# An interleaved local and block attention kernel: stacks, local scores and half-chunk sums each moved in fewer DMAs, in an order found anew

## The chip, the cores and the metric

The kernel runs on one core of one Trainium2 chip. A core has a TensorE (PE in the profile; its weight loads are listed apart as PEld), a VectorE (DVE), a ScalarE (ACT), a GpSimd (POOL) and a SyncE (SP). In this kernel SP issues most DMAs and ACT the rest; each of the two has a DMA queue of its own, and all transfers run on the core's 16 DMA engines. The metric is the device time of one execution in microseconds (us), as the median of several runs.

## What is computed

Four layers work in turn on x (2048 rows of 512, float32): A, B, A, B. Each is x + attention(layernorm(x)), with 32 heads of 16.

```python
def _A_ref(x, wqkv, wo):            # W, dil = 8, 2
    idx = pos[:, None] - off[None, :]        # off = arange(8) * 2
    ...
    logits = jnp.einsum("bhsd,bhswd->bhsw", q, kg) * scale
    attn = _softmax(logits, axis=-1)
    o = jnp.einsum("bhsw,bhswd->bhsd", attn, vg)

def _B_ref(x, wqkv, wo):            # W = 256
    scores = jnp.einsum("bhqd,bhkd->bhqk", q, k) * (Dh ** -0.5)
    mask = (idx[:, None] - idx[None, :] >= 0) & (idx[:, None] - idx[None, :] < W)
    p = _softmax(jnp.where(mask[None, None], scores, -1e9), axis=-1)
    o = jnp.einsum("bhqk,bhkd->bhqd", p, v)

x = x + _A_ref(_layernorm(x), A_wqkv, A_wo)
x = x + _B_ref(_layernorm(x), B_wqkv, B_wo)
x = x + _A_ref(_layernorm(x), A_wqkv, A_wo)
x = x + _B_ref(_layernorm(x), B_wqkv, B_wo)
```

## The kernel before

**Tiles and stages.** The 2048 rows are worked in 8 chunks of 256 (C = 256), so that the four layers make 16 A-chunks and 16 B-chunks. They are interleaved: while one B-chunk computes its scores on PE, the next A-chunk is projected and scored.

**An A-chunk** projects Q and K, computes the scores of 39 neighbouring rows for each group (`WIN` = 39) in two halves, and ScalarE copies each half from PSUM to a tile `s` of 128 x 1248 float32 (L1202). `shelve` (L1211) writes `s` to a DRAM tile `sd`, and `band` (L1215) reads it back along a diagonal into the tile `l`, where only the 8 wanted neighbours of each row are left. The probabilities go over DRAM too (`ptd`, `ptt`, L1285) before they meet V.

**A B-chunk** projects K, then Q, each in two halves. ScalarE takes a high float16 part `eh` from PSUM (L1331) and VectorE the remainder `el` (L1334). These have 128 partitions (4 groups of 32) with even and odd heads apart. To multiply high and low parts in one pass, the rows of a head's high, low and high part must lie in neighbouring partitions, so they are sorted anew through a DRAM tile `re`: six writes for K and six for Q in each B-chunk (`put`, L1344, 128 KB each), and then reads into the stacks `stk_q` (L1357) and `stk_k` (L1359). There are four stacks of Q and four of K in a chunk (`j` = 0 to 3, a pair of half `hf` and quarter `hp`); each is two DMAs of 48 rows, for even and odd heads, and waits for all six writes of its side. Rows 48 to 63 and 112 to 127 of the stacks are pads, written once at the start by 12 DMAs (`stk_k<-pad`, `stk_q<-pad`); two rows of the pads of Q are filled in every chunk with the maxima of the scores (`md`, L1471 and L1477).

The first scores, on 48 rows (L1404 in the first chunk of a layer, L1420 after), only serve to find the maxima on VectorE (L1435). The second (L1571), on 64 rows, contain the maxima as a subtraction, so that ScalarE takes their exponential straight from PSUM (L1581, L1593). GpSimd masks (L1610), PE multiplies by V with a column of ones (L1626), and the sums `os` hold each head's output and its denominator. `gather` (L1700) fetches the denominators of a half chunk into `rc`, VectorE inverts them, `scr` (L1710) and `os` (L1715) spread them over DRAM, and `gather_o` (L1705) fetches the outputs into `oc`.

**What sets the order.** Every piece of work is a task of the planner: an engine, a duration, a function that emits its instructions, and the values that it reads and writes. The dictionary `ORDER` gives each task of a chunk ("A0", "B0", and so on) a place; a negative place puts it on its other engine, which for DMAs is ACT for SP. Each engine gets its tasks sorted by place, the planner lays them out against each other by its own durations, and the instructions are emitted in that order. On the chip each engine executes its list strictly in that order: a DMA that waits for its data keeps back all that stands behind it on SP or ACT, and a matmul that waits keeps back all of PE. The planner gives a DMA a cost by its bytes alone, `dma = max(dma, t.end + 0.9) + t.size / 390.0`. At the start, PE also runs `IDLE` = 122 groups of matmuls that compute nothing (L1763).

Of the kernel before, what the change touches and what calls it, by code (L numbers as in the profile page):

```python
# [18 lines left out]
P = 128  # L19
S = 2048  # L20
# [660 lines left out]
def kernel(  # L681
# [456 lines left out]
    def layer_a(l, c):  # L1138
# [42 lines left out]
        for t in range(2):  # L1181
# [18 lines left out]
            for i in range(2):  # L1200
                def keep(i=i, S_=S_, pbs=pbs):
                    nc.scalar.copy(S_.t.rearrange("p k (s r) -> p r s k", r=4)[:, 2 * i : 2 * i + 2],  # L1202
                                   pbs[i].t[:, :, 0 : 8 * WIN].rearrange("p r (s k) -> p r s k", s=8))

                plan.add("ACT", 1.15, keep, r=[vpb[i]], w=[vS[i]])
            sd = buf("dram", [4, 32 * (WIN + 1) * H], F32, "sd", f"sd{l}_{c}_{t}")
            vsd = Val(sd)

            def shelve(E, S_=S_, sd=sd):
# [595 lines left out]
```

## Time and profile before

| what | before |
|---|---|
| time, median of 3 runs | 1408.19 us (1407.26 to 1411.21) |
| the profiled execution | 1414.15 us, of which the span of the profile is 1412.4 us |
| granted TensorE clock in it | 0.974 |
| PE matmul / weight load busy | 93% / 60% |
| DVE, ACT, POOL busy | 60%, 58%, 29% |
| DMA traffic | 195.08 MB in 203658 packets, mean 138 GB/s |

The profile covers one execution. In the chain of work that ended last, each step is followed back to what released it; "SPq" and "ACTq" are the times that the sequencers of SP and ACT took to issue a DMA, "DMA" the time from issue to landing. In a timeline, a row gives the start in us, the duration in us, the engine, the line of the kernel, the operation and its tiles as out<-in, and how many instructions are summed in the row; what an instruction waited for stands in square brackets. In a table of windows there is, for each stretch, the busy time and number of instructions of each engine, then the granted clock, the mean busy share of the 16 DMA engines, and GB/s.

### The profile page before, as it was taken

How to read it: one execution, taken by the hardware profiler on the slowest of the kernel's cores; microseconds unless marked ns; L12 is line 12 of the kernel's file. 1: busy time of each engine (PE TensorE's matmuls, PEld its weight loads, DVE VectorE, ACT ScalarE, POOL GpSimd, SP SyncE). 2: the span in 40 equal slices, each digit the busy share in tenths (PEclk: the TensorE clock that was granted, in tenths of full speed). 3: DMA queues.
4: the chain of work that ended last, by engine and by line, in shares of the span. 5: the costliest groups of instructions: out<-in, count | busy, mean ns of one | idle time of the engine just before them, and what ended most of it. 6: DMA issues, size and time to landing. Idle time of an engine off the chain costs nothing.

```text
span 1412.4 us, 62375 instructions
## 1 busy us (share of the span) xinstructions
PE 1308.5 (93%) x27206; PEld 841.8 (60%) x27206; DVE 852.2 (60%) x1932; ACT 825.8 (58%) x1303; POOL 405.9 (29%) x839
## 2 busy tenths in 40 slices
PE   8989999999898999879999898989999898998988
PEld 7766556575475746646566464746656474574645
DVE  5455764755647666374664637566473765748494
ACT  7754657474574746546676373838557364663644
POOL 5260212332221233133223130323242241222232
PEclk9999999999899998999999999999999999999999
DMA  8875544736355373552545546364554636335332
GB/s 261 236 168 162 133 115 135 154 114 171 102 148 134 88 200 92 148 147 86 160 113 152 152 143 158 94 174 125 157 123 134 175 100 155 102 98 147 103 98 67
DMA packets 203658, 195.08 MB, mean 138 GB/s; under 512 B 92892, under 2 KB 147932, under 8 KB 203384
## 3 DMA queue, kind: packets, MB, share of 16 engines
q1 hardware_dynamic: 175096, 170.43, 44.2%
q10 hardware_dynamic: 28288, 20.66, 6.0%
q8 instruction: 213, 3.49, 1.1%
q14 instruction: 61, 0.50, 0.1%
HBM read 94.11 MB, written 79.36 MB: 123 GB/s over the span
## 4 chain that ended last, share of the span: by engine, by line
PE 59%; DMA 11%; DVE 10%; ACT 7%; SPq 4%; issue 4%; POOL 2%; ACTq 1%; DVEq 0%; POOLq 0%
PE banks L1034 7%; PE banks L1626 7%; PE banks L1035 6%; PE banks L1036 6%; PE banks L1056 5%; PE banks L1054 5%; PE banks L1571 4%; PE banks L1057 4%; PE banks L1420 4%; DVE m L1435 3%; PE banks L1193 3%; PE banks L1302 3%; ACT p L1581 2%; DMA stk_q<-re 2%; DVE banks L1439 1%
## 5 line engine op out<-in xcount | busy, mean ns | idle before, releaser
L1435 DVE TENSOR_REDUCE m<-banks 128x2 f32<-128x512 f32 x448 | 302.1, 688 | 8.4
L1581 ACT ACTIVATE p<-banks,sclB 128x896 f32<-128x896 f32 x224 | 221.0, 1007 | 74.3 <-PE banks L1571 51.5
L1439 DVE COPY_PREDICATED banks<-trm,banks 128x128 f32<-128x128 int16 x448 | 124.2, 291 | 120.8 <-PE banks L1420 111.8
L1610 POOL TENSOR_SCALAR_AFFINE_SELECT ps<-ps 64x256 f32<-64x256 f32 x300 | 118.2, 416 | 252.3 <-ACT ps L1593 231.2
L1610 POOL TENSOR_SCALAR_AFFINE_SELECT p<-p 64x256 f32<-64x256 f32 x264 | 103.1, 412 | 214.7 <-ACT p L1581 206.6
L1420 PE MATMUL banks<-stk_k,stk_q 48*64 48x320 f16 (+4 forms) x2560 | 139.5, 274 | 24.5 <-DVE m L1435 7.0
L1571 PE MATMUL banks<-stk_q,stk_k 64*64 64x256 f16 (+3 forms) x3584 | 121.0, 239 | 25.0 <-DMA stk_q<-md 8.4
L1420 PEld LDWEIGHTS <-stk_q 48*64 48x64 f16 x2560 | 65.7, 107 | 107.5 <-issue 94.8
L1571 PEld LDWEIGHTS <-stk_k 64*64 64x64 f16 x3584 | 70.3, 108 | 91.0 <-issue 74.3
L1593 ACT ACTIVATE ps<-banks,sclB 128x768 f32<-128x768 f32 x112 | 100.2, 899 | 40.7 <-PE banks L1571 28.4
L1626 PE MATMUL banks<-p,v 64*32 64x192 f32 (+1 forms) x3584 | 112.6, 355 | 6.1 <-ACT p L1581 1.8
L1202 ACT COPY s<-banks 128x624 f32<-128x624 f32 x64 | 74.7, 1257 | 40.7 <-PE banks L1193 23.1
L1640 DVE TENSOR_TENSOR os<-os,banks 128x256 f32<-128x256 f32 x112 | 45.7, 416 | 83.4 <-ACT os L1643 67.0
L1334 DVE SCALAR_TENSOR_TENSOR el<-banks,eh 128x512 f16<-128x512 f32 x64 | 42.8, 687 | 79.4 <-ACT eh L1331 74.0
L1626 PEld LDWEIGHTS banks<-p,v 64*32 64x32 f32 x3584 | 62.9, 106 | 37.6 <-issue 13.0
L1643 ACT COPY os<-banks 128x256 f32<-128x256 f32 x112 | 40.8, 370 | 70.6 <-PE banks L1626 54.4
L1034 PE MATMUL banks<-xh,wA1h 128*128 128x256 f16 x256 | 72.1, 282 | 4.1 <-ACT v L1369 4.1
L1034 PE MATMUL banks<-xh,wA0h 128*128 128x256 f16 x256 | 71.9, 281 | 0.6 <-ACT v L1369 0.6
L1035 PE MATMUL banks<-xl,wA1h 128*128 128x256 f16 x256 | 71.7, 280 | 0.0
L1036 PE MATMUL banks<-xh,wA1l 128*128 128x256 f16 x256 | 71.5, 279 | 0.0
L1035 PE MATMUL banks<-xl,wA0h 128*128 128x256 f16 x256 | 71.3, 279 | 0.0
L1036 PE MATMUL banks<-xh,wA0l 128*128 128x256 f16 x256 | 71.1, 278 | 0.0
(216 smaller groups left out, 3063.8 us busy)
## 6 DMA issues: line engine op xcount, KB each, us to landing
sd<-s SPq DMA_DIRECT2D x92, 156.0 KB
ptt<-ptd SPq DMA_DIRECT2D x128, 96.0 KB
stk_k<-re SPq DMA_DIRECT2D x128, 96.0 KB
stk_q<-re SPq DMA_DIRECT2D x128, 96.0 KB
vs<-vd SPq DMA_DIRECT2D x64, 156.0 KB
re<-eh SPq DMA_DIRECT2D x75, 128.0 KB
vd<-ve SPq DMA_DIRECT2D x32, 256.0 KB
xm<-y SPq DMA_DIRECT2D x32, 256.0 KB
```

What stands on the lines that cost most here:

```text
L1034: nc.tensor.matmul(ps[mp].t[:, i], wh, xh, start=k == 0, stop=False)
L1035: nc.tensor.matmul(ps[mp].t[:, i], wh, xl, start=False, stop=False)
L1036: nc.tensor.matmul(ps[mp].t[:, i], wl, xh, start=False, stop=k == 3)
L1202: nc.scalar.copy(S_.t.rearrange("p k (s r) -> p r s k", r=4)[:, 2 * i : 2 * i + 2], pbs[i].t[:, :, 0 : 8 * WIN].rearrange("p r (s k) -> p ...
L1420: nc.tensor.matmul(o, lhs, k, start=True, stop=True, tile_position=(64 * par, 64 * h))
L1435: nc.vector.tensor_reduce(out=m.t[:, :, u, qb], in_=ps.t[:, :, 0 : 2 * P], op=ALU.max, axis=AX.X)
L1439: nc.vector.copy_predicated(t[:, :, 0:64], trm[:, 0].bitcast(I16).unsqueeze(1).broadcast_to([P, 2, 64]), t[:, :, C : C + 64])
L1571: nc.tensor.matmul(ps.t[64 * h : 64 * h + 64, par, at + x0 : at + x0 + q1 - q0], stk[hf, kt][r, col, k0 : k0 + 64], stk[hf, 0][r, col, q0: ...
L1581: nc.scalar.activation(big.t[:, 2 * i : 2 * i + 2], ps.t[:, :, 0:448], AF.Exp, scale=scl["B", 1])
L1593: nc.scalar.activation(small.t.rearrange("p (i m) x -> p m i x", i=2), ps.t[:, :, 0:384].rearrange("p m (i x) -> p m i x", i=2), AF.Exp, s ...
L1610: E.affine_select(out=v, in_=v, pattern=[[0, 4], [a, 64]], compare_op=op, fill=0.0, base=0, channel_multiplier=-a)
L1626: nc.tensor.matmul(acc.t[32 * mm : 32 * mm + 32, h, q0:q1], vv[r, 17 * (H * blk + hd) : 17 * (H * blk + hd) + 32], x.t[r, mm, x0 : x0 + q1 ...
```

## The change

Three transfers and their order are changed; what PE computes stays the same.

- **Stacks and pads.** The DRAM tile `re` of 3 parts by 2 halves becomes a ring of three permanent tiles for Q and three for K, of 4 stacks x 2 (even, odd) x 64 rows x 1024. Rows 48 to 63 of each hold the pads, written once at the start (6 DMAs in place of 12). A stack is one DMA of 128 rows with the pads (256 KB) in place of two of 48 rows (96 KB each). The writes of `put` are as many as before (12 in a B-chunk, 128 KB each), but what was in DRAM 64 rows of 2 pieces is now 4 stacks of 32 pieces.
- **Local scores.** `shelve` writes all 128 rows in one DMA instead of four of 32; `band` reads them in two DMAs instead of one, with a source of 4 x 16 rows.
- **A half chunk's sums.** `gather` is one DMA with a source of 4 x 16 x 64 in place of four of 16 x 64; the write of `scr` becomes two.
- **Order.** All places of `ORDER` (and the list `RECORDS`) are new; some tasks change engines. Counted over the orders of SP and ACT, SP has some 209 DMAs less and ACT 64 less, of about 1376.

The diff, without the tables:

```diff
 ORDER = {
-    "A0": [0, 1, 0, 1, 2, 3, 4, 5, 6, 5, 27, 11, 5, 6, 26, 9, 6, 15, 42, 46, 48, 49, 53, 54, 55, 56, 43, 44, 45, 47,
+    "A0": [1, 0, 2, 3, 0, 1, 4, 5, 6, 4, 21, 6, 2, 5, 25, 8, 7, 15, 43, 46, 47, 48, 49, 53, 56, 57, 42, 44, 45, 50, 51,
...
-            sd = buf("dram", [4, 32 * (WIN + 1) * H], F32, "sd", f"sd{l}_{c}_{t}")
+            sd = buf("dram", [P, WIN * H], F32, "sd", f"sd{l}_{c}_{t}")
             def shelve(E, S_=S_, sd=sd):
-                for g in range(4):
-                    E.dma_start(sd.t[g, 0 : 32 * WIN * H].rearrange("(q x) -> q x", q=32), S_.t[32 * g : 32 * g + 32].rearrange("p k s -> p (k s)"))
+                E.dma_start(sd.t, S_.t.rearrange("p k s -> p (k s)"))
             def band(E=nc.sync, t=t, sd=sd):
                 x = sd.t
-                E.dma_start(L.t[64 * t : 64 * t + 64].rearrange("p u w s -> p u (w s)"),
-                                  bass.AP(tensor=x.tensor, offset=x.offset, ap=[[2 * (WIN + 1) * H, 64], [(WIN + 1) * H, 2], [1, W * H]]))
+                for u in range(2):
+                    E.dma_start(L.t[64 * t : 64 * t + 64, u].rearrange("p w s -> p (w s)"),
+                                  bass.AP(tensor=x.tensor, offset=x.offset + u * (WIN + 1) * H, ap=[[32 * WIN * H, 4], [2 * (WIN + 1) * H, 16], [1, W * H]]))
...
-            re = buf("dram", [4, 16, 3, 2, 2, 2 * C], F16, f"e{s}", f"re{l}_{c}_{s}")
-            vre = [[Val(re) for _ in range(3)] for _ in range(2)]
+            n3 = (l // 2 * NCH + c) % 3
+            re, vre, vedge = far_e[s, n3], vfar[s, n3], vpads[s, n3]
                     def put(E, z=z, n=n, par=par, re=re, e=e):
-                        E.dma_start(re.t[:, :, z, par].rearrange("q c u x -> (q c) u x"),
+                        E.dma_start(re[:, par, 16 * z : 16 * z + 16].rearrange("q c (u x) -> q (c u) x", u=2),
                                           e[n].t[:, par].rearrange("p i t -> p (i t)"))
...
                 def stack(E=nc.sync, j=j, s=s, re=re, hp=hp, t=stk[hf, i]):
-                    src = re.t.rearrange("q c z f u x -> q f (c z) (u x)")
-                    for par in range(2):
-                        x = t[64 * par : 64 * par + 48, 4 * hp : 4 * hp + 4]
-                        if s == 0:
-                            E.dma_start(x.rearrange("p a t -> p (a t)"), src[j, par])
-                        else:
-                            E.dma_start(x, src[j, par].rearrange("p (a t) -> p a t", a=4))
-                plan.add("SP", 1.3, stack, r=vre[0] + vre[1], w=[vst[hf, i, hp]], size=225 if s else 192)
+                    x, src = t[:, 4 * hp : 4 * hp + 4], re[j].rearrange("f r x -> (f r) x")
+                    if s == 0:
+                        E.dma_start(x.rearrange("p a t -> p (a t)"), src)
+                    else:
+                        E.dma_start(x, src.rearrange("p (a t) -> p a t", a=4))
+                plan.add("SP", 0.65, stack, r=[*vre[0], *vre[1], vedge], w=[vst[hf, i, hp], *([] if s else [vst[hf, "m", hp]])], size=290 if s else 256)
...
             def gather(E, hf=hf):
                 s_ = flat(os_[hf])
-                for m in range(4):
-                    s = 16 * (2 * m + hf)
-                    E.dma_start(rc.t[s : s + 16, 0], s_[32 * m + 16 : 32 * m + 17].rearrange("m (k f) -> m k f", f=64))
+                E.dma_start(rc.t[64 * hf : 64 * hf + 64, 0], s_[16::32].rearrange("m (k f) -> m k f", f=64))
-        plan.add("SP", 0.4, lambda: nc.sync.dma_start(scr.t.rearrange("m (k f) -> (m k) f", f=64), rc.t[:, 1]), r=[vrr], w=[vscr], size=32)
+        def sums_out(E=nc.sync):
+            for hf in range(2):
+                E.dma_start(scr.t[hf::2].rearrange("m (k f) -> m k f", f=64), rc.t[64 * hf : 64 * hf + 64, 1])
+        plan.add("SP", 0.8, sums_out, r=[vrr], w=[vscr], size=32)
...
+    far_e = {(s, i): far.tile([4, 2, 64, 4 * C], F16, name=f"re{s}_{i}") for s in range(2) for i in range(3)}
+        for i in range(3):
+            def put(i=i, k=min(some[0], 1), pad=pad):
+                nc.sync.dma_start(far_e[k, i][:, :, 48:64].rearrange("q f r x -> r (q f) x"), zeros(pad).unsqueeze(1).broadcast_to([16, 8, 4 * C]))
```

How the order of instructions changes is shown at two engines in one place, the third B-chunk of the last layer (chunk 10 of 16). A row is the line, the operation, the tiles (with their numbers; the digits name layer, chunk and side, K being `_1` and Q `_0` in `re_2_1` and `re_2_0`) and the shape written, then how many alike follow each other. Lines after the change are one to three lower for the same statement.

**SP** before, from the first write of K to the reads of the stacks and local scores:

```order
L1344 DMA re_2_1_16579<-eh_2_1_16509 64x2x512
L1344 DMA re_2_1_16579<-el_2_1_16547 64x2x512 x2
L1477 DMA stk_q<-md_1_3_16559 2x1024 x2
L1344 DMA re_2_1_16579<-eh_2_1_16509 64x2x512
L1359 DMA stk_k<-re_2_1_16579 48x4x256 x2
L1344 DMA re_2_0_16731<-eh_2_0_16675 64x2x512 x3
L1344 DMA re_2_0_16731<-el_2_0_16685 64x2x512 x2
L1211 DMA sd_3_0_16809<-s_3_0_16733 32x1248 x4
L1357 DMA stk_q<-re_2_0_16731 48x1024 x2
L1359 DMA stk_k<-re_2_1_16579 48x4x256 x2
```

and SP now, in the same place:

```order
L1468 DMA md_1_3_16310<-mt_1_3_16283 4x32x32 x2
L1343 DMA re_1_176<-eh_2_1_16375 4x32x512
L1474 DMA stk_q<-md_1_3_16310 2x1024 x2
L1343 DMA re_1_176<-eh_2_1_16375 4x32x512
L1343 DMA re_1_176<-el_2_1_16384 4x32x512
L1124 DMA xm_2_16030<-y_2_0_15650 128x512
L1356 DMA stk_k<-re_1_176 128x4x256
L1343 DMA re_1_173<-eh_2_0_16481 4x32x512 x3
L1343 DMA re_1_173<-el_2_0_16519 4x32x512
L1356 DMA stk_k<-re_1_176 128x4x256
L1209 DMA sd_3_0_16609<-s_3_0_16526 128x1248
L1354 DMA stk_q<-re_1_173 128x1024 x3
```

The four DMAs of `sd` and the pairs of the stacks have become one each; three reads of Q's stacks follow each other, and the second read of K's stacks stands ahead of the first of Q's, no longer behind it. The writes of `re` are of the form 4x32x512 now, the form that the writes of `md` had before and have still.

**ACT** before, at the same chunk, where it takes over a part of the writes:

```order
L1344 DMA re_2_1_16579<-eh_2_1_16509 64x2x512
L1165 ACTIVATE qm_3_16370<-banks,half 128x16x32 x2
L961 ACTIVATE unread,mv_5_16447<-x_5_1_16505,mv_5_16447 128x512
L1593 ACTIVATE ps_1_4_16670<-banks,sclB_170 128x2x2x192
L1331 ACTIVATE eh_2_0_16675<-banks 128x2x256
L996 CAST ht_4_1_16680<-xn_4_1_16380 128x512
L1331 ACTIVATE eh_2_0_16675<-banks 128x2x256
L1202 COPY s_3_0_16733<-banks 128x2x8x39
L1344 DMA re_2_0_16731<-eh_2_0_16675 64x2x512
L1202 COPY s_3_0_16733<-banks 128x2x8x39
L1202 COPY s_3_1_16814<-banks 128x2x8x39 x2
L961 ACTIVATE unread,mv_5_16447<-x_5_0_15694,mv_5_16447 128x512
```

and ACT now:

```order
L1343 DMA re_1_176<-eh_2_1_16375 4x32x512 x2
L1164 ACTIVATE qm_3_16195<-banks,half 128x16x32 x2
L1343 DMA re_1_176<-el_2_1_16384 4x32x512
L1695 DMA rc_1_16435<-os_1_0_15932 64x1x64
L1330 ACTIVATE eh_2_0_16481<-banks 128x2x256 x2
L1201 COPY s_3_0_16526<-banks 128x2x8x39
L1343 DMA re_1_173<-eh_2_0_16481 4x32x512
L1343 DMA re_1_173<-el_2_0_16519 4x32x512
L1201 COPY s_3_0_16526<-banks 128x2x8x39
L1201 COPY s_3_1_16605<-banks 128x2x8x39 x2
L1209 DMA sd_3_1_16640<-s_3_1_16605 128x1248
```

ACT issues one write of Q and one of K more than before in this chunk, with the denominators of a half chunk (`rc`) in one DMA between them, and its two activations of `eh` for Q follow each other without a cast between.

More of the change, by code (lines that the diff above doesn't have):

```diff
@@ L41 @@
 ORDER = {
[397 rows of a table removed]
[396 rows of a table added]
 }
-RECORDS = "15:1 40:1 67:1 151:1 275:1 316:-1 317:2 322:1 323:-1 470:1 473:1 492:2 526:2 538:1 550:1 572:1 643:1 675:1 715:1 716:-1 721:-1 722:1 762:1 843:2 892:1 905:1 955:1 986:1 1039:1 1051:1 1190:-1 1191:1 1196:-1 1197:3 1367:1 1473:1 1514:1 1585:1 1665:2 1666:-1 1671:2 1672:-1 1830:1 1911:1 1936:1 1952:2 2140:1 2141:-1 2146:-1 2147:2 2183:1 2187:1 2305:1 2411:2 2423:1 2535:1 2615:-1 2616:1 2621:-1 2622:2 2662:1 2758:1 2780:1 2792:1 2808:1 2833:1 2861:1 2886:1 2939:1 3018:1 3090:2 3091:-1 3096:2 3097:-1 3320:1 3414:1 3426:1 3564:1 3565:-1 3570:2 3571:-1 3729:2 3741:1 3754:1 3782:1 3794:1 3835:1 3847:1 3959:1 4040:-1 4041:2 4046:-1 4047:2 4087:1 4194:1 4204:2 4228:1 4262:1 4296:1 4379:1 4439:3 4440:-1 4445:3 4446:-1 4486:1 4576:1 4604:1 4616:1 4626:1 4657:1 4722:1 4729:1 4775:1 4842:1 4914:1 4915:-1 4920:-1 4921:2 4961:1 5079:1 5091:1 5185:1 5250:1 5337:1 5389:1 5390:-1 5395:2 5396:-1 5436:1 5520:1 5554:1 5619:1 5623:1 5691:1 5713:1 5864:2 5865:-1 5870:2 5871:-1 5907:1 6041:1 6082:1 6147:1 6287:1 6299:1 6339:1 6340:-1 6345:2 6346:-1 6382:1 6516:1 6523:1 6569:1 6579:1 6610:1 6622:1 6635:1 6663:1 6675:1 6754:1 6814:1 6815:-1 6820:-1 6821:2 6861:1 6991:1 7044:1 7150:1 7288:2 7289:-1 7294:2 7295:-1 7453:1 7470:1 7490:1 7518:1 7535:1 7561:1 7583:1 7632:1 7665:1"
@@ new lines @@
+RECORDS = "15:1 40:1 67:1 148:1 235:1 275:1 316:-1 317:2 322:1 323:-1 470:1 482:1 526:1 538:1 675:1 715:1 716:-1 721:1 722:-1 758:1 843:1 892:1 905:1 986:1 1039:1 1051:1 1190:-1 1191:2 1196:2 1197:-1 1355:1 1367:1 1408:1 1420:1 1473:1 1514:1 1526:1 1665:1 1666:-1 1671:-1 1672:3 1708:1 1830:2 1842:1 1858:1 1883:2 1936:1 1989:1 2068:1 2140:-1 2141:2 2146:2 2147:-1 2183:1 2305:1 2317:1 2358:1 2370:1 2411:1 2423:1 2464:1 2543:1 2615:2 2616:-1 2621:-1 2622:3 2758:1 2780:1 2792:1 2814:1 2833:2 2870:1 2898:1 2939:1 3090:2 3091:-1 3096:-1 3097:2 3137:1 3320:1 3361:1 3426:1 3485:1 3564:2 3565:-1 3570:-1 3571:2 3611:1 3741:1 3782:1 3804:1 3900:2 3959:1 4040:2 4041:-1 4046:2 4047:-1 4087:1 4228:1 4296:1 4367:1 4439:2 4440:-1 4445:3 4446:-1 4576:1 4604:1 4616:1 4657:1 4775:1 4854:1 4914:-1 4915:2 4920:2 4921:-1 4961:1 5079:1 5091:1 5185:2 5250:1 5337:1 5389:1 5390:-1 5395:-1 5396:2 5523:1 5554:1 5566:1 5570:1 5619:1 5623:1 5672:1 5713:1 5725:1 5864:1 5865:-1 5870:2 5871:-1 6029:1 6094:1 6147:1 6339:-1 6340:1 6345:-1 6346:2 6382:1 6482:1 6504:1 6516:1 6520:1 6557:1 6591:1 6675:1 6754:1 6773:1 6814:2 6815:-1 6820:2 6821:-1 6857:1 6979:1 6991:1 7138:1 7150:1 7209:1 7288:-1 7289:2 7294:1 7295:-1 7437:1 7453:1 7470:1 7490:1 7518:1 7583:1 7600:1 7632:1 7648:1"
@@ L1205, in layer_a @@
                 plan.add("ACT", 1.15, keep, r=[vpb[i]], w=[vS[i]])
-            sd = buf("dram", [4, 32 * (WIN + 1) * H], F32, "sd", f"sd{l}_{c}_{t}")
+            sd = buf("dram", [P, WIN * H], F32, "sd", f"sd{l}_{c}_{t}")
             vsd = Val(sd)
             def shelve(E, S_=S_, sd=sd):
-                for g in range(4):
-                    E.dma_start(sd.t[g, 0 : 32 * WIN * H].rearrange("(q x) -> q x", q=32), S_.t[32 * g : 32 * g + 32].rearrange("p k s -> p (k s)"))
+                E.dma_start(sd.t, S_.t.rearrange("p k s -> p (k s)"))
             def band(E=nc.sync, t=t, sd=sd):
                 x = sd.t
-                E.dma_start(L.t[64 * t : 64 * t + 64].rearrange("p u w s -> p u (w s)"),
-                                  bass.AP(tensor=x.tensor, offset=x.offset, ap=[[2 * (WIN + 1) * H, 64], [(WIN + 1) * H, 2], [1, W * H]]))
-            plan.add("SP", 2.4, shelve, r=vS, w=[vsd], size=600, alt=("ACT", 2.4))
-            plan.add("SP", 0.65, band, r=[vsd], w=[vL[t]], size=160)
+                for u in range(2):
+                    E.dma_start(L.t[64 * t : 64 * t + 64, u].rearrange("p w s -> p (w s)"),
+                                  bass.AP(tensor=x.tensor, offset=x.offset + u * (WIN + 1) * H, ap=[[32 * WIN * H, 4], [2 * (WIN + 1) * H, 16], [1, W * H]]))
+            plan.add("SP", 0.65, shelve, r=vS, w=[vsd], size=600, alt=("ACT", 0.65))
+            plan.add("SP", 1.2, band, r=[vsd], w=[vL[t]], size=160)
         if c == 0:
@@ L1705, in gather_o @@
                     E.dma_start(o.t.rearrange("p g t -> p (g t)")[2 * m + hf :: 8], s_[32 * m : 32 * m + 16])
-            plan.add("SP", 2.6, gather, r=vos[hf], w=[vrc[hf]], size=8, alt=("ACT", 2.7))
+            plan.add("SP", 0.65, gather, r=vos[hf], w=[vrc[hf]], size=8, alt=("ACT", 0.7))
             plan.add("SP", 2.5, gather_o, r=vos[hf], w=[vog[hf]], size=256, alt=("ACT", 2.65))
         plan.add("DVE", 0.47, lambda: nc.vector.reciprocal(rc.t[:, 1], rc.t[:, 0]), r=vrc, w=[vrr])
-        plan.add("SP", 0.4, lambda: nc.sync.dma_start(scr.t.rearrange("m (k f) -> (m k) f", f=64), rc.t[:, 1]), r=[vrr], w=[vscr], size=32)
+        def sums_out(E=nc.sync):
+            for hf in range(2):
+                E.dma_start(scr.t[hf::2].rearrange("m (k f) -> m k f", f=64), rc.t[64 * hf : 64 * hf + 64, 1])
+        plan.add("SP", 0.8, sums_out, r=[vrr], w=[vscr], size=32)
         vbc = Val(os_[1])
@@ L1731 @@
     prep("B")
+    far_e = {(s, i): far.tile([4, 2, 64, 4 * C], F16, name=f"re{s}_{i}") for s in range(2) for i in range(3)}
+    vfar = {k: [[Val() for _ in range(3)] for _ in range(2)] for k in far_e}
+    vpads = {k: Val() for k in far_e}
     def zeros(pad):
-        return pad.t.rearrange("p a b -> p (a b)").bitcast(F16)
+        return pad.t.rearrange("p a b -> p (a b)").bitcast(F16)[0:16, 0 : 4 * C]
     for some in ((0,), (1, 2)):
@@ L1741, in fill @@
             v = zeros(pad)
-            nc.gpsimd.memset(v[0:16, 0:C], 0.0)
+            nc.gpsimd.memset(v, 0.0)
             if some[0]:
-                nc.gpsimd.memset(v[0:2, 0:C], -MC)
+                nc.gpsimd.memset(v[0:2], -MC)
         plan.add("POOL", 0.5, fill, w=[vpad])
-        for hf in range(2):
-            for i in some:
-                def put(hf=hf, i=i, pad=pad):
-                    for par in range(2):
-                        nc.sync.dma_start(stk[hf, i][64 * par + 48 : 64 * par + 64], zeros(pad)[0:16, 0:C].unsqueeze(1).broadcast_to([16, 8, C]))
-                plan.add("SP", 1.3, put, r=[vpad],
-                         w=[vst[hf, i, 0], vst[hf, i, 1], *([] if i else [vst[hf, "m", 0], vst[hf, "m", 1]])], size=64)
+        for i in range(3):
+            def put(i=i, k=min(some[0], 1), pad=pad):
+                nc.sync.dma_start(far_e[k, i][:, :, 48:64].rearrange("q f r x -> r (q f) x"), zeros(pad).unsqueeze(1).broadcast_to([16, 8, 4 * C]))
+            plan.add("SP", 0.65, put, r=[vpad], w=[vpads[min(some[0], 1), i]], size=256)
     plan.begin("W")
```

789 rows, old and new, of the table ORDER are left out of this document.

## The prediction

> **What bounds the kernel now.** I read the page's busy times first, then its chain of work that ended last, then the groups by line.
>
> ```profile
> PE 1308.5 (93%) x27206; PEld 841.8 (60%) x27206; DVE 852.2 (60%) x1932; ACT 825.8 (58%) x1303; POOL 405.9 (29%) x839
> PE 59%; DMA 11%; DVE 10%; ACT 7%; SPq 4%; issue 4%; POOL 2%; ACTq 1%; DVEq 0%; POOLq 0%
> L1420 PE MATMUL banks<-stk_k,stk_q 48*64 48x320 f16 (+4 forms) x2560 | 139.5, 274 | 24.5 <-DVE m L1435 7.0 <-ACT ps L1593 3.8 <-DMA stk_q<-re 3.5
> L1571 PE MATMUL banks<-stk_q,stk_k 64*64 64x256 f16 (+3 forms) x3584 | 121.0, 239 | 25.0 <-DMA stk_q<-md 8.4 <-DVE m L1435 5.4 <-ACT os L1643 3.8
> L1571 PEld LDWEIGHTS <-stk_k 64*64 64x64 f16 x3584 | 70.3, 108 | 91.0 <-issue 74.3 <-DMA stk_q<-md 11.1 <-DMA sd<-s 0.7
> L1420 PEld LDWEIGHTS <-stk_q 48*64 48x64 f16 x2560 | 65.7, 107 | 107.5 <-issue 94.8 <-DMA stk_q<-re 6.7 <-DMA sd<-s 0.6
> ```
>
> PE is the bound: it is idle for 1412.4 - 1308.5 = 104 us, 6.5 us in each of 16 chunks. So hardly any time is to be had by speeding up other engines, and every microsecond by which PE's next operand comes later is new time, unless it falls into those 6.5. DMA is 11% of the chain and the issuing of DMAs 4% + 1%, or 71 us: that is what fewer DMAs can touch. PE waits for the stacks already: 3.5 + 8.4 + 11.1 + 6.7 = 29.7 us, 1.9 in a chunk.
>
> How tight the stacks are is seen in the timelines: SP's queue in chunk 8, the same in ACT's queue and on PE, and then chunk 10.
>
> ```profile
> 748.76 0.56 SPq L1344 DMA_DIRECT2D re<-eh  x1
> ...
> 757.25 0.56 SPq L1344 DMA_DIRECT2D re<-el  x1
> ...
> 761.83 0.85 SPq L1357 DMA_DIRECT2D stk_q<-re  x2
> ```
> ```profile
> 757.67 0.55 ACTq L1344 DMA_DIRECT2D re<-el  x1
> ```
> ```profile
> 766.43 0.23 PE L1404 MATMUL banks<-stk_k,stk_q 48*128 48x128 f16 x2
> ```
> ```profile
> 906.12 0.55 SPq L1344 DMA_DIRECT2D re<-eh  x1
> ...
> 914.89 1.82 SPq L1344 DMA_DIRECT2D re<-eh  x3
> 916.75 1.32 SPq L1344 DMA_DIRECT2D re<-el  x2
> 918.18 2.85 SPq L1211 DMA_DIRECT2D sd<-s  x4
> 921.19 1.08 SPq L1357 DMA_DIRECT2D stk_q<-re  x2
> ```
> ```profile
> 926.79 0.24 PE L1420 MATMUL banks<-stk_k,stk_q 48*64 48x128 f16 x1 [2.07 <-DMA stk_q<-re]
> ```
>
> Twelve writes of `re` go out within 9 to 12 us, the last of Q's (757.67, 916.75) a few us ahead of the first read of a Q stack (761.83, 921.19); 4.6 to 5.6 us after that read is issued PE uses it, in chunk 10 after waiting 2.07 us for it. So there is no slack: what delays the writes of `re` delays PE.
>
> **The change part by part: issuing.** Durations are minimum/median/maximum in ns.
>
> ```profile
> L1211 SPq DMA_DIRECT2D sd<-s x92: 302/422/1503, 37.5 to 1272.5; - x92
> L1357 SPq DMA_DIRECT2D stk_q<-re x128: 302/413/1876, 118.5 to 1350.0; - x128
> L1359 SPq DMA_DIRECT2D stk_k<-re x128: 308/436/1938, 114.5 to 1350.9; - x128
> L1700 SPq DMA_DIRECT2D rc<-os x72: 502/589/1667, 190.8 to 1324.0; - x72
> L1215 SPq DMA_DIRECT2D l<-sd x32: 536/564/1676, 42.4 to 1280.3; - x32
> ```
>
> By the order of the changed kernel SP issues 74 fewer `sd` (74 x 0.422 = 31 us), 64 and 64 fewer stacks (26 + 28 us) and 61 fewer `rc` (36 us); it issues 32 more `l` (18 us). That is over 100 us of SP's time, but SP is not the bound. In the whole, 273 of some 1376 DMAs go, 20%, so of the 71 us of issuing on the chain I take 20%: **14 us** gained. The ends are nothing (all of it beside PE's work) and twice that, 28 us, if the removed fours and pairs stood on the chain twice as often as others.
>
> **Bytes of the stacks.** A stack moves 256 KB in one DMA, not 192 in two. At 18.4 GB/s for each of 16 engines (worked out below) the 65.5 KB more take 0.22 us, and the second issue of 0.41 us is saved ahead of the landing: no net cost, between -0.2 and +0.2 us a stack. The Q stack now overwrites the rows of `md` as well; their readers are the matmuls of L1571 that read the other rows of the same tile, so that wait was there before. The pads are written once at the start.
>
> **The form of the writes.** The writes of `re` stay 192 of 128 KB, but their DRAM side is 4x32x512 instead of 64x2x512. What that does is seen in another write of that form, `md`, L1471 (4x32x32). ACT's queue and what ACT issues:
>
> ```profile
> q10 hardware_dynamic: 28288, 20.66, 6.0%
> ```
> ```profile
> re<-eh ACTq DMA_DIRECT2D x53, 128.0 KB
> ...
> sd<-s ACTq DMA_DIRECT2D x36, 156.0 KB
> ...
> re<-el ACTq DMA_DIRECT2D x20, 128.0 KB
> oc<-os ACTq DMA_DIRECT2D x40, 64.0 KB
> ...
> ptd<-bands ACTq DMA_DIRECT2D x13, 144.0 KB
> ...
> rc<-os ACTq DMA_DIRECT2D x48, 4.0 KB
> md<-mt ACTq DMA_DIRECT2D x40, 8.0 KB
> ...
> oc<-os ACTq DMA_DIRECT2D x8, 32.0 KB
> ```
>
> The pieces that the shapes make are 73 x 128 for `re`, 36 x 32 for `sd`, 13 x 576 for `ptd`, 40 x 128 for `md`, 48 x 16 each for `oc` and `rc`: 24640. The queue counts 28288 packets, 3648 more. If each DMA adds one packet on each engine that it runs on (a mark of its end), 258 DMAs on 16 engines would add 4128; 480 = 12 x 40 are missing. So 40 of them run on 4 engines, not 16. By number `oc` would do as well as `md`, but `md` is the one that is cut into 4. **A DMA whose slowest part counts 4 runs on 4 engines**, and that is now the form of all writes of `re`, of the sources of `l` and `rc`, and of the writes of `scr`.
>
> Are they the same four each time? Four reads `ptt` of 24 rows stood alone in the queue, after this row:
>
> ```profile
> 1292.32 1.74 SPq L1285 DMA_DIRECT2D ptt<-ptd  x4
> ```
> ```profile
> 748.00:758.00 10.00, 10.00 (x278) 7.96 (x275) 3.65 (x6) 5.38 (x8) 0.66 (x1) 1.00 0.59 174
> 758.00:766.00 8.00, 8.00 (x193) 4.03 (x191) 0.42 (x1) 6.62 (x8) 1.50 (x3) 1.00 0.80 218
> 1293.60:1294.00 0.40, 0.40 (x2) 0.03 (x2) 0.40 (x1) 0.17 (x1) 0.35 (x2) 1.00 0.66 200
> 1294.00:1294.40 0.40, 0.40 (x17) 0.31 (x16) 0.37 (x2) 0.00 (x0) 0.40 (x2) 1.00 0.66 215
> ```
>
> The last two columns are the busy share of the 16 engines and GB/s. With four transfers in flight the share stays at 0.66, below the 12/16 = 0.75 that they would give if each ran on the same twelve (24 rows shared out evenly, two to an engine), where mixed traffic reaches 0.80. I take them as the same.
>
> [...]
>
> The price of one write: an engine moves 215 / (16 x 0.66) = 20.4 GB/s in the last window, 174 / (16 x 0.59) = 18.4 in the first. On four engines 131 KB take 131 / (4 x 20.4) = **1.61 us**, or 1.78 us; on 16 they take 0.40 to 0.45. Twelve take 19.3 to 21.4 us, one behind the other, where all twelve took about 5. In chunk 8 they begin at 748.76 + 0.56 = 749.3 and end at 768.6 to 770.7, while the first Q stack's read went out at 761.83: 6.8 to 8.9 us late. In chunk 10, from 906.7, they end at 926.0 to 928.1 against 921.19: 4.8 to 6.9 late. The mean of the four is **6.9 us** in a chunk. The Q stack waits on SP for that long, and behind it stand, by the order, the other Q stacks, two `l` and a K stack, all of which PE or VectorE need next.
>
> What of it hides: the 1.9 us in which PE waits for stacks already, and, since the other engines catch up while PE stands, a third of the remaining 4.6 us of idle time, 1.5. That third is a choice; the ends are nothing and all of it. Left are 6.9 - 3.4 = 3.5 us, x 16 = **56 us**.
>
> **Smaller ones.** Two `l` of 64 KB on four engines take 65.5 / 81.6 = 0.8 us each in place of 0.4 together: 1.2 us more in each half of an A-chunk, on VectorE's path, which is busy 60%. I take nothing, with an upper end of 2 x 1.2 x 16 = 38 us. `rc` and `scr` are 4 to 16 KB; their pieces on four engines cost less than the three issues that go: nothing.
>
> **The sum.** 1414.15 + 56 - 14 = 1456 us for an execution like the profiled one. That lies 0.42% above the median of the runs (1408.19 / 1414.15 = 0.9958), so **1450 us** as a median.
>
> **The rivals.**
> 1. *Faster: the late writes are covered and the issues decide.* PE idles 6.5 us a chunk, and in chunk 10 the writes are late by 4.8 us at the lower price; if all the idle time is filled, nothing is left of 4.8, and 14 us are gained: 1400, or 1394 as a median. It decides when the lateness less what it hides is under 14 / 16 = 0.9 us a chunk. For it speaks that the new order issues the first writes of K with less ahead of them; against, that PE waits for this very stack before (2.07 us in chunk 10). The same time comes out if the change does not do what its shapes say, the 4x32x512 being cut again to 16 shares; the unchanged `md` speaks against. Together 0.17.
> 2. *The narrow writes run on different engines each time.* Then they go beside each other, only the last one is late, by 1.61 - 0.40 = 1.2 us, 19 us in 16 chunks, less 14: 1419, or 1413. The windows at 0.66 speak against. 0.12, two thirds of it within the noise.
> 3. *SP becomes the bound.* While a Q stack waits on SP, the `l` and the next rows behind it wait too, PE stands again at the local chunk, and nothing is hidden: 6.9 x 16 = 110, to 8.9 x 16 = 142, less 14: 1510 to 1542, 1504 to 1535 as a median. For it speaks the strict order on SP; against, that SP has over 100 us less to issue. 0.10.
>
> **How the numbers follow.** The forecast has 0.61. Its own range goes from 4.8 late with 4 hidden (+13 - 14) to 8.9 with only 1.9 hidden (+112 - 14): 1408 to 1506. The range takes that in, and half of rival 1 with its gain of up to 28 us: 1390 to 1508; left out are the rest of rival 1 and most of rival 3. A measurement of this kernel tells 0.3% (4 us) from no change. Faster 0.17; within 0.3% 0.09 (two thirds of rival 2 and the very bottom of the forecast); slower 0.74.
>
> **What would show it.** In the changed profile: writes of `re` that land 5 to 10 us after their issue in a burst; PE's waits for `stk_q<-re` growing from 10 us to over 60 in all; the chain's DMA share rising from 11% and SPq falling below 4%; PE's busy time still near 1308 us in a longer span; the packets of ACT's queue 12 fewer for each write of `re`. The prediction is wrong if `re` writes still land within 2 to 3 us, or if PE's idle time stays near 104 us; the step at fault would then be the four engines, or the share that hides.

## The result, and the profile after

| | before | after |
|---|---|---|
| time, median of 4 runs each | 1407.72 us | 1540.57 us (1536.7 to 1546.4) |
| ratio | 1 | 1.0952 (95% interval 1.0895 to 1.1008) |
| span of the profile | 1412.4 us | 1542.0 us |
| PE idle in the span | 104 us | 190 us |
| granted clock | 0.974 | 0.932 |

The change makes the kernel 9.5% slower. That it would be slower was forecast, the size was not: 1450 us was the forecast and 1508 the upper end of the range. The busy times and the chain of the page after:

```profile
PE 1351.7 (88%) x27206; PEld 855.4 (55%) x27206; DVE 855.6 (55%) x1937; ACT 826.1 (54%) x1300; POOL 395.4 (26%) x810
q10 hardware_dynamic: 26480, 23.27, 5.5%
PE 44%; DMA 30%; DVE 8%; SPq 7%; ACT 6%; issue 3%; POOL 1%; ACTq 0%; DVEq 0%; POOLq 0%
DMA re<-el 9%; DMA re<-eh 6%; PE banks L1623 6%; PE banks L1055 5%; PE banks L1417 4%; PE banks L1053 4%; PE banks L1033 4%; PE banks L1056 4%; PE banks L1034 4%; PE banks L1035 4%; PE banks L1568 3%; DVE m L1432 3%; DMA stk_q<-re 3%; PE banks L1301 2%; DMA sd<-s 2%
```

DMAs hold 30% of the chain instead of 11%, and the writes of `re`, of which no line stood among the first before, lead it with 9% + 6% of 1542 us, some 230 us. The 129.6 us by which the span grew are 86 us more of PE standing idle and 43 us more of PE being busy, the same 27206 matmuls, which ran at a lower clock (0.932 against 0.974, shown below).

What PE waits for, by the view of waits (us in all, times, longest):

```profile
PE banks L1417 <- DMA stk_q<-re: 55.2, 15, 8.9
PE banks L1568 <- DVE el L1333: 18.5, 4, 5.9
PE banks L1055 <- DVE el L1333: 15.6, 6, 4.8
PE banks L1401 <- DMA stk_q<-re: 8.2, 2, 4.9
```

The Q stacks (3.5 us at L1420 before) and, new, the low parts `el`. Chunk 8 in SP's queue, from K's first write to the first Q stack, and behind it the chain in the same place:

```profile
811.50 0.54 SPq L1343 DMA_DIRECT2D re<-eh  x1
...
823.17 1.23 SPq L1343 DMA_DIRECT2D re<-eh  x2
824.44 0.92 SPq L1343 DMA_DIRECT2D re<-el  x1
...
834.75 0.35 SPq L1354 DMA_DIRECT2D stk_q<-re  x1
```
```profile
819.90 1.31 PE banks L1623 x48
821.20 1.08 ACT eh L1330 x2
...
824.44 10.11 DMA re<-el
...
834.75 2.96 DMA stk_q<-re
...
837.75 0.50 PE banks L1401 x4
```

The last write of Q lands 10.1 us after its issue and the stack is read at once; PE follows 3 us later. From K's first write to the read of the stack it is 834.75 - 811.50 = 23.2 us, where it was 761.83 - 748.76 = 13.1. A second thing shows in the view of the tile `eh`, at what the engines that write or read it waited for (us, times):

```profile
  DMA re<-eh: 72.8, 11
  DMA re<-el: 65.1, 11
```

In the same view before these rows read 5.1 us (once) and 1.1 us (once); waits of ScalarE and of VectorE are both in them. The kernel's pool `pqk` has two buffers in all for `eh` and `el`, and K's two parts fill them. So Q's parts can be taken from PSUM only when K's writes of `re` have read those buffers: K's slow writes put off Q's conversion as well.

### The profile page after: what moved, and what is told of

Its sections match the earlier page's. It is cut to its first block, busy times and chain, and to the rows that moved or that the text cites. A ratio compares the mean times of both kernels' runs of the same rounds, so it can differ in the third digit from the quotient of the medians.

```text
span 1542.0 us, 62052 instructions
## 1 busy us (share of the span) xinstructions
PE 1351.7 (88%) x27206; PEld 855.4 (55%) x27206; DVE 855.6 (55%) x1937; ACT 826.1 (54%) x1300; POOL 395.4 (26%) x810
## 3 DMA queue, kind: packets, MB, share of 16 engines
q1 hardware_dynamic: 178216, 176.96, 42.4%
q10 hardware_dynamic: 26480, 23.27, 5.5%
## 4 chain that ended last, share of the span: by engine, by line
PE 44%; DMA 30%; DVE 8%; SPq 7%; ACT 6%; issue 3%; POOL 1%; ACTq 0%; DVEq 0%; POOLq 0%
DMA re<-el 9%; DMA re<-eh 6%; PE banks L1623 6%; PE banks L1055 5%; PE banks L1417 4%; PE banks L1053 4%; PE banks L1033 4%; PE banks L1056 4%; PE banks L1034 4%; PE banks L1035 4%; PE banks L1568 3%; DVE m L1432 3%; DMA stk_q<-re 3%; PE banks L1301 2%; DMA sd<-s 2%
## 5 line engine op out<-in xcount | busy, mean ns | idle before, releaser
L1607 POOL TENSOR_SCALAR_AFFINE_SELECT p<-p 64x256 f32<-64x256 f32 x276 | 108.4, 415 | 302.4 <-ACT p L1578 298.3
L1568 PE MATMUL banks<-stk_q,stk_k 64*64 64x128 f16 (+3 forms) x3584 | 124.7, 244 | 39.3 <-DVE el L1333 18.5
L1607 POOL TENSOR_SCALAR_AFFINE_SELECT ps<-ps 64x256 f32<-64x256 f32 x252 | 98.7, 414 | 217.1 <-ACT ps L1590 190.9
L1623 PE MATMUL banks<-p,v 64*32 64x192 f32 (+1 forms) x3584 | 118.5, 369 | 7.7 <-DVE p L1601 4.5
L1330 ACT ACTIVATE eh<-banks 128x512 f16<-128x512 f32 x64 | 36.6, 597 | 97.0 <-DMA re<-eh 48.0
L1033 PE MATMUL banks<-xh,wB1h 128*128 128x256 f16 x256 | 70.0, 273 | 0.8 <-DVE xl L1017 0.3
L1623 PE MATMUL banks<-ps,v 64*32 64x64 f32 (+1 forms) x3584 | 70.2, 255 | 0.5 <-issue 0.5
```

What stands on the lines that cost most here:

```text
L1033: nc.tensor.matmul(ps[mp].t[:, i], wh, xh, start=k == 0, stop=False)
L1568: nc.tensor.matmul(ps.t[64 * h : 64 * h + 64, par, at + x0 : at + x0 + q1 - q0], stk[hf, kt][r, col, k0 : k0 + 64], stk[hf, 0][r, col, q0: ...
L1607: E.affine_select(out=v, in_=v, pattern=[[0, 4], [a, 64]], compare_op=op, fill=0.0, base=0, channel_multiplier=-a)
L1623: nc.tensor.matmul(acc.t[32 * mm : 32 * mm + 32, h, q0:q1], vv[r, 17 * (H * blk + hd) : 17 * (H * blk + hd) + 32], x.t[r, mm, x0 : x0 + q1 ...
```

## The experiments

Each ratio is to the kernel before, run beside it on the same chip, with its 95% interval.

**Are the narrow writes the cause?** One run widens them in the changed kernel, one narrows them in the kernel before. In the first the tile `re` is laid out so that each write is one contiguous block. The one read of a stack then has a source of 8 x 16 rows, and the pads are written in 12 DMAs instead of 6 (of each diff here the main lines are shown):

```diff
-far.tile([4, 2, 64, 4 * C], F16, name=f"re{s}_{i}")
+far.tile([2, 4, 4, 16, 4 * C], F16, name=f"re{s}_{i}")
-E.dma_start(re[:, par, 16 * z : 16 * z + 16].rearrange("q c (u x) -> q (c u) x", u=2),
+E.dma_start(re[par, z].rearrange("q c (u x) -> (q c u) x", u=2),
-x, src = t[:, 4 * hp : 4 * hp + 4], re[j].rearrange("f r x -> (f r) x")
+x, src = t[:, 4 * hp : 4 * hp + 4], re[:, :, j].rearrange("f z c x -> (f z) c x")
...
```

> The changed kernel with one thing altered: the DRAM tile re is laid out so that each write is contiguous (128x512, as in the form on 16 engines), and the one read of a stack has a source of 8x16 rows. Order, issues, local scores and sums stay as changed. Theory (the narrow writes make the loss): the time falls by more than 100 us, to 1390 to 1430; landing of re<-eh near 2.5 us, PE idle near 104 us, clock near 0.97. Rival (the new order makes it): it stays above 1500. Rival (the other narrow forms, l, rc, scr): stays above 1480.

Measured: 1412.35 us, 1.0004 (0.9978 to 1.0029), clock 0.975. The loss is gone, as the theory said.

```profile
PE 1307.1 (92%) x27206; PEld 840.9 (59%) x27206; DVE 855.4 (60%) x1937; ACT 826.4 (58%) x1300; POOL 395.2 (28%) x810
```

PE's busy time is back too. The second run, in the kernel before:

```diff
-re = buf("dram", [4, 16, 3, 2, 2, 2 * C], F16, f"e{s}", f"re{l}_{c}_{s}")
+re = buf("dram", [4, 2, 48, 4 * C], F16, f"e{s}", f"re{l}_{c}_{s}")
-E.dma_start(re.t[:, :, z, par].rearrange("q c u x -> (q c) u x"),
+E.dma_start(re.t[:, par, 16 * z : 16 * z + 16].rearrange("q c (u x) -> q (c u) x", u=2),
-src = re.t.rearrange("q c z f u x -> q f (c z) (u x)")
+src = re.t
```

> The kernel before with one thing altered: the DRAM side of the writes of re is 4x32x512 instead of 64x2x512; two reads of 48 rows per stack, the old order and everything else stay. Theory (the narrow writes): slower by 100 us or more, 1500 to 1550, PE idle near 190 us, clock near 0.93. Rival (the order, the stacks in one, SP's queue): within 20 us of 1408.

Measured: 1547.2 us, 1.0947 (1.0899 to 1.0994), clock 0.943. The same 128 KB in the same number of DMAs, only cut 4x32x512, makes a loss of the same size by itself.

```profile
PE 1342.3 (87%) x27206; PEld 853.6 (55%) x27206; DVE 852.9 (55%) x1932; ACT 824.6 (54%) x1303; POOL 405.5 (26%) x839
```

**Is it the new order?** The changed kernel with the table of places and the records of before:

> The changed kernel with the table of places and the records of before (the last eight places of pB, for the pads, those of the changed one). Theory (the narrow writes): still 1500 to 1560. Rival (the new order makes the loss): 1390 to 1430.

Measured: 1536.36 us, 1.0870 (1.0814 to 1.0927). That is 0.8% less than the change's 1.0952, with intervals that overlap: the order is not the cause.

**How the writes add up.** The changed kernel with K's six writes widened as above and Q's left narrow:

> The changed kernel with K's writes of re wide (16 engines, K's stacks read on 8) and Q's six as changed, on 4. Theory (one queue: K's six run out before Q's begin, and what PE waits for are Q's six): most of the loss stays, 1490 to 1530. Rival (all twelve add up, as the prediction had it, so that half of them gone takes away more than the lateness of 7 us less 6 x 1.6 = 10 us): 1400 to 1440.

Measured: 1481.93 us, 1.0548 (1.0496 to 1.0601), under the range of the first theory and above that of the rival. Both sixes count. The starts of the writes of `re` and of the first read of a Q stack, in each of the 16 B-chunks of five traces, show how (means in us):

```
                  K's first write  Q's last write   K's first write
                  to Q's first     to the read      to the read
before                  8.0             3.7              14.8
after                  11.6             8.7              24.8
K wide, Q narrow        7.8             9.8              20.4
both wide               7.8             3.8              14.2
before_narrow          11.7             7.2              23.4
```

With K's writes narrow Q's first write comes 3.6 us later, and with K's wide it does not, which fits the waiting for buffers; with Q's narrow the read comes 3.5 to 6 us later after the last of them. In all the stack is read 10.0 us later in each chunk after the change.

**The clock.** After one of the new waits the trace shows the lower clock directly. PE waits 4.52 us for `el` in chunk 10, and the same form of matmul takes 0.63 us behind the wait instead of 0.38; in the table of windows the granted clock (third column from the end) is 0.50 for 6 us behind it:

```profile
992.18 0.38 PE L1056 MATMUL banks<-wB3l,oh 128*128 128x512 f16 x1
997.30 0.58 PE L1055 MATMUL banks<-wA2h,xh 128*128 128x512 f16 x1 [4.52 <-DVE el L1333]
1002.03 0.63 PE L1056 MATMUL banks<-wB3l,oh 128*128 128x512 f16 x1
```
```profile
992.80:997.20 4.40, 0.00 (x0) 0.00 (x0) 0.64 (x2) 2.18 (x3) 0.00 (x0) 0.95 0.23 80
997.30:1003.30 6.00, 6.00 (x137) 3.17 (x137) 0.55 (x1) 3.51 (x3) 0.00 (x0) 0.50 0.37 106
1003.30:1006.30 3.00, 3.00 (x107) 1.73 (x105) 0.00 (x0) 0.00 (x0) 0.00 (x0) 0.96 0.80 236
```

How short a wait of PE leaves the granted clock as it was, was not measured here.

Two runs fill the waits. In front of the first score of a B-chunk, where PE waits for the Q stack, they put 36 matmuls that compute nothing:

```diff
+                        if fresh:
+                            fresh.clear()
+                            v = idf.bitcast(F16)
+                            for _ in range(36):
+                                nc.tensor.matmul(ps.t[:, 0, 0 : 2 * P], v[:, 0:P], v, start=True, stop=True)
```

In a first run they stood in front of the score that is first by number:

> The changed kernel with 36 matmuls that compute nothing (some 4 us) in front of the first score of each B-chunk on PE, where it stands waiting for a Q stack; nothing else. Theory (the clock is granted lower because PE stands idle there): the granted clock rises from 0.932 towards 0.97, the program's matmuls take 20 to 40 us less in all, and the time falls by 10 to 40 us although work was added. Rival (the lower clock has another cause, or is a cause and not a result): clock within 0.01, time the same or up to 30 us longer.

Measured: 1604.11 us, 1.1361, clock 0.939. By the trace the waits for Q stacks at these scores (L1425 in this kernel) stayed at 50.2 us: in most chunks another score is executed first, so the idle matmuls came behind the wait and mostly added their time. PE was busy for 1411.4 us, of which they took 60.4 + 10.7 us; the kernel's own matmuls took 1340.3 us, 11 us less than in the changed kernel. The second run puts them in front of whichever score comes first:

> As the run with 36 idle matmuls, but they stand in front of whichever score PE executes first in a B-chunk; the earlier run had them in front of the first by number, which PE often reaches later, past its wait, so that they added 64 us. Theory (idle time lowers the granted clock): PE's wait for the Q stack falls by 30 us or more, clock 0.95 to 0.975, time 1500 to 1540. Rival (the clock falls for another reason): clock within 0.01 of 0.932, time 1540 to 1560, since the added work fills the wait.

Measured: 1548.72 us, 1.1051 (1.0995 to 1.1107), clock 0.955.

```profile
PE 1397.3 (90%) x27782; PEld 906.1 (58%) x27782; DVE 855.1 (55%) x1937; ACT 826.2 (53%) x1300; POOL 394.7 (25%) x810
```
```profile
L1415 PE MATMUL banks<-idf 128*128 128x256 f16 x504 | 57.6, 273 | 0.1
L1396 PE MATMUL banks<-idf 128*128 128x256 f16 x72 | 8.2, 273 | 0.0
```

The idle matmuls took 65.8 us, so the kernel's own were busy for 1397.3 - 65.8 = 1331.5 us, 20 us less than in the changed kernel and 9 us less than in the first run, which left the waits unfilled. The granted clock was 0.955 to 0.963 in the four executions, against 0.932 to 0.938 in the changed kernel and 0.939 to 0.947 in the first run. So the idle time does lower the clock in this kernel; how much of the 43 us is owed to these waits alone the two runs don't settle. The time did not fall to 1500 to 1540 us as I had expected; it lies where the rival had it. The 65.8 us of filling took only 36 us off PE's idle time (190 to 154 us) and 20 us off its own matmuls.

**Where the expected gain is.** With wide writes the changed kernel is as fast as before, not faster. The sums alone, in the kernel before (`gather` in one, `scr` in two):

> The kernel before with the half chunk's sums alone as changed: one gather in place of four, scr in two (some 75 DMAs fewer); old order. Theory A (issuing was not on the path that PE bounds): within 0.3% of before. Theory B (fewer issues gain): 0.3% to 0.7% faster, 4 to 10 us, since SP and ACT spend some 47 us less.

Measured: 1382.49 us, 0.9875 (0.9830 to 0.9919), more than either expectation. And the local scores as well:

> The kernel before with the sums and the local scores as changed (some 140 DMAs fewer; l on 4 engines), stacks, writes of re and order as before. Theory A: within 0.4% of before. Theory B (issues gain): 0.5% to 1% faster, 7 to 14 us. Rival C (the narrow reads of l cost): 0.5% slower or more.

Measured: 1374.45 us, 0.9813 (0.9768 to 0.9859): faster than both kernels of this study, and again by more than expected. The narrow reads of `l` cost nothing that shows beside the gain.

```profile
PE 1293.0 (94%) x27206; PEld 836.9 (61%) x27206; DVE 850.7 (62%) x1932; ACT 826.9 (60%) x1303; POOL 407.0 (30%) x839
```

Of the 42 us between this profiled span (1370.1 us) and that of the kernel before, 15 are PE's matmuls at a higher clock (0.989) and 27 its idle time.

Where the sums' gain of some 20 us may come from is seen in the view of the tile `rc` in the kernel before, at who waited for it (us, times):

```profile
  ACT ht L996: 9.8, 1
  ACT xn L986: 8.4, 2
  ACT mt L1458: 7.3, 1
  ACT ve L1264: 6.0, 2
  ACT ps L1593: 5.5, 1
  ACT v L1369: 3.1, 1
```

These are 40 us of ScalarE's arithmetic that ended behind gathers which ACT itself was issuing; none of it needs `rc`. Not all of the 40 us is the gathers' own, since a wait is put down to what ended it. The longest, with the kernel before first and the run with one gather second:

```profile
348.74 5.83 ACTq L1705 DMA_DIRECT2D oc<-os  x4
354.61 0.67 ACTq L1278 DMA_DIRECT2D ptd<-bands  x1
355.31 2.66 ACTq L1700 DMA_DIRECT2D rc<-os  x4
358.01 0.62 ACT L996 CAST ht<-xn 128x512 f16<-128x512 f32 x1 [9.75 <-DMA rc<-os]
```
```profile
343.68 4.54 ACTq L1703 DMA_DIRECT2D oc<-os  x4
348.27 0.65 ACTq L1278 DMA_DIRECT2D ptd<-bands  x1
349.35 0.62 ACTq L1698 DMA_DIRECT2D rc<-os  x1
350.01 0.62 ACT L996 CAST ht<-xn 128x512 f16<-128x512 f32 x1 [6.81 <-DMA oc<-os]
```

The four DMAs of `oc` ahead made most of this wait, and it shrank from 9.75 to 6.81 us. With one gather 0.2 us of ACT's waits are left under `rc`, but the rest of a wait like this one stands under `oc` now. What ACT surely saves is issuing: 48 x 0.601 = 29 us became 12 x 0.613 = 7 us. Two runs split the gathers by the issuing engine, `if E is nc.scalar` one DMA and otherwise four, and the other way round; the write of `scr` is two DMAs in both:

> As before_gather (0.9875 of before), but only the 12 gathers that ACT issues are one DMA; the 18 of SP stay four of 16 rows. Theory (the gain came from ACT, whose arithmetic stands behind its own DMAs: in the profile of before it waits some 40 us on rc, in that of before_gather under 1): 0.985 to 0.992. Rival (it is the number of DMAs, 54 of the 90 removed being SP's): 0.994 to 0.998.

Measured: 1399.47 us, 0.9920 (0.9890 to 0.9950), at the edge of the theory's range.

> The other half: only the 18 gathers that SP issues are one DMA, ACT's 12 stay four. Theory (ACT's part makes the gain): 0.996 to 1.003. Rival (number of DMAs): 0.990 to 0.994.

Measured: 1413.39 us, 0.9996 (0.9968 to 1.0025). The 36 DMAs that ACT is spared gain 0.8%, the 54 that SP is spared nothing that can be measured. The two don't quite add up to 1.25%, within their intervals.

**What takes that gain away with wide writes.** The changed kernel with stacks, pads and writes of `re` as before, and then wide writes with the old order:

> The changed kernel with stacks, pads and writes of re as before (two reads of 48 rows on 16 engines, 64x2x512 writes); new order, local scores and sums as changed. If the stack in one read on 8 engines ate a gain in the run with wide writes: 0.4% to 1% faster than before, 1398 to 1406. If there was no gain to eat: within 0.4% of before. If the new order needs the shorter issues: slower by 0.5% to 1%.

Measured: 1398.9 us, 0.9973 (0.9943 to 1.0004).

> The changed kernel with wide writes of re (as in after_wide: writes on 16 engines, each stack one read on 8) and the table of places and records of before (the last eight places of pB those of the changed one). Its difference to before_both (0.981 of before) is the single read of a stack on 8 engines; its difference to after_wide (1.000) is the new order. If the new order costs the gain: 0.975 to 0.985. If the single stack on 8 engines costs it: 0.995 to 1.005. If both do, half each: about 0.99.

Measured: 1408.75 us, 1.0026 (0.9998 to 1.0053). All these kernels have the sums and the local scores as changed. Against before_both (0.9813), the stacks as changed, with wide writes, cost 2.1%, and the new order with the old stacks 1.6%; but with the wide writes both orders are alike (1.0004 and 1.0026). The two costs don't add. Of the stacks' cost it is not shown which part makes it: one read in place of two, on 8 engines in place of 16, of 256 KB with the pads in place of 192 KB. That it is 8 engines fits SP's queue: with wide writes it counts 178692 packets, 476 more than the changed kernel's 178216, which is 12 more for each of 117 writes, 8 fewer for each of 128 stack reads, and 96 more for the pads (12 DMAs of 80 packets, not 6 of 144). In the wide kernel the view of PE's waits still has

```profile
PE banks L1417 <- DMA stk_q<-re: 25.4, 12, 4.5
```

A stack in one read on 16 engines together with wide writes was not tried.

## Why the prediction was right and wrong

- **The narrow form of the writes: right.** ACT's queue after the change has pieces of 75 x 128 (`re`), 14 x 32 x 4 (`sd`), 12 x 576 (`ptd`), 38 x 128 (`md`), 36 x 16 (`oc`) and 19 x 64 (`rc`), 24960 in all; the other 1520 of 26480 packets are 4 for each of 132 DMAs (`re`, `md`, `rc`) and 16 for each of the other 62. That settles that `md`'s form, and not `oc`'s, was the narrow one. The two runs agree: with wide writes the queue counts 27380 packets, 12 more for each of the 75 writes, and in before_narrow 27412, 12 fewer than before for each of 73. That they run on the same four fits twelve writes that take over 22 us in chunk 8 (811.50 + 0.54 to 834.55); which four they are, no view shows.
- **The lateness: the first step that failed, by its size.** Twelve writes at 1.61 to 1.78 us were to make the stack 6.9 us late; it is read 10.0 us later. That is 3.1 us a chunk, 50 us in all. In chunk 8 the price comes to 22.5 / 12 = 1.9 us, above the 1.78; other transfers on the four engines may be why, which no run shows. And K's writes hold the buffers that Q's conversion needs, 3.6 us of the 10.0, a wait that the prediction did not name.
- **The clock: the second step that failed, put at nothing.** "PE's busy time still near 1308 us" was wrong: it is 1351.7 us, and 43 of the 130 us are matmuls at the lower clock. That it follows the waits is shown by the rows above, by the run with wide writes (1307.1 us) and, in part, by the filled waits. The 50 us and these 43 make 93 us; the measured time lies 91 us above the forecast. That the two close the gap is arithmetic, not a run, and a part of the lateness may itself come from the lower clock.
- **What hides: near in size, wrong in its make-up.** The sum let 3.4 us a chunk vanish, and 0.9 for issuing, 4.3 together. Of the 10.0 us PE's idle time shows 86 / 16 = 5.4, so 4.6 did not come as idle time. In the two pairs that differ in the writes (the second also in the engines of the stack reads) it is 2.8 us (before and before_narrow: 8.6 later, idle 104 and 197 us) and 5.6 us (both wide and after: 10.7 later, idle 109 and 190 us); no run shows what took it up. But the "1.9 us in which PE waits for stacks already" were misread: they add PEld's waits to PE's, whose 3.5 + 8.4 us all lie inside those of PEld, and most of them are for `md`. From K's first write to its first score PE stood idle for only 0.8 us a chunk before, and 8.3 after; outside these stretches it was 5.7 a chunk before and 3.6 after.
- **14 us for issuing: not shown.** It was 20% of all issuing on the chain, from 273 of 1376 DMAs; the trace counts 1604 that SP and ACT issue (1346 + 258, without 60 transposes), which would give 17% and 12 us. What there is comes to 26 us in the old order. Of the sums' 1.25% some 0.8% comes from the DMAs that ACT issues, and nothing measurable from SP's 54; the local scores were not split. With the stacks as changed none of it is left. "SPq falling below 4%" was wrong as well; it is 7%.
- **`l` on four engines at no cost, `rc` and `scr` at none:** before_both shows no cost beside its gain (0.9813). Its SP queue counts 1360 packets fewer than that of before_gather (172536 and 173896), which is 16 for each of 69 `sd` less, and 4 for each of 64 `l` in place of 16 for each of 32.
- **Rival 3** came nearest in time (1504 to 1535) by taking nothing as hidden, but its mechanism is not what the trace has: PE waits for Q stacks and `el`, hardly for what stands behind the stacks on SP. It too put the clock at nothing, so its nearness is luck.
- **Rivals 1 and 2** fell: the late writes were not covered, since PE stands idle for 86 us more, and the writes did not go beside each other, since twelve took 22.5 us in chunk 8.

## What to carry to other kernels

Before merging DMAs or laying out a DRAM tile anew, look at the outer count of each access pattern that results: a write whose outer part counts 4 ran on a quarter of the engines here (12 packets fewer for each in ACT's queue), and with twelve of them in a burst the kernel lost 9.5%, while the DMAs saved were worth 1.9% at best. A late operand of the bounding engine cost twice here, by the time that the engine stood and by the clock that fell with it, from 0.974 to 0.932: 10.0 us of lateness a chunk became 5.4 us of idle time and 2.7 us of slower matmuls. Count the buffers that a slow transfer holds, too: Q's first write came 3.6 us later by them. Try first to merge the DMAs that a computing engine issues: its arithmetic stood behind them here (36 DMAs fewer on ACT gained 0.8%), while merging SP's gathers gained nothing that could be measured (0.9996).

## What was not expected of the hardware

- Standing idle for 86 us more went with a granted clock of 0.932 instead of 0.974, and the same matmuls took 43 us longer, half as long as the added idle time; behind a wait of 4.52 us the clock was 0.50 for 6 us.
- Twelve narrow writes went one behind the other in chunk 8, at some 1.9 us each, where the prediction had 0.40 to 0.45 us for one in the old form.
- Merging ACT's 48 gathers of 4 KB, whose issuing takes 0.6 us each, into 12 gained 0.8%; merging SP's 72 into 18 gained nothing measurable.
